# Long convolution, modulation and mixer MLP on one core: last inverse stage split per PSUM buffer, gelu table loaded early, loads regrouped on one queue, all tasks in a new order

## The chip, the core and the metric

The kernel runs on one core of a Trainium2 chip. A core has a matmul engine (TensorE, PE in the profile), a vector engine (VectorE, DVE), a scalar engine with function tables (ScalarE, ACT), a general engine (GpSimd, POOL) and a sync engine that issues transfers (SyncE, SP). Each engine works through its own queue in order; they wait for each other by semaphores. Matmuls write to PSUM, and ACT or DVE carries the results from there to SBUF, which is called eviction here. Transfers are issued from SP or POOL and carried by 16 DMA engines. The metric is the device time of one execution in microseconds (us), less is better.

## The reference

Everything is bf16, with S = 2048 positions and D = 640 channels. `rfft2` and `irfft2` over axes (1, 2) with one of them of length 1 are FFTs of length 2S along the positions.

```python
mod = (_silu(c) @ w_mod).reshape(c.shape[0], 6, 1, -1)
sa, ca, ga, sb, cb, gb = (mod[:, i] for i in range(6))
h = _layernorm(x) * (1 + ca) + sa              # x = A_q
x = x + ga * A(h, k, v)
h = _layernorm(x) * (1 + cb) + sb
x = x + gb * B(h)

def A(q, k, v):
    kv = shift(k, shift_k) * v                 # causal filter of 4 taps along S
    y = irfft(rfft(kv, 2 * S) * rfft(ssm_k, 2 * S))[:S]
    return q * (y + kv * ssm_D)

def B(x):
    h = gelu(_layernorm(x) @ w1)
    hs = concat(four quarters of h, shifted by +1, -1, +2, -2 positions) @ w2
    x1 = x + hs
    return x1 + gelu(_layernorm(x1) @ w3) @ w4     # w3: 640 x 1728
```

## The kernel before

**Stages.** The positions form 16 tiles of 128. The convolution is an FFT of length 4096 done with matmuls, in five blocks of 128 channels. A first stage with a 32-point matrix (`stage1`, matmuls L407) and a second with a 64-point matrix (`stage2_half`, matmuls L427) transform the filter (called s, result in R3) and the product kv (result in R5). In front of it stand the tables of sines, loads with transposes of k and v, and the filter of four taps by matmuls (L463). `inverse1` multiplies the two spectra on DVE (20 products of 128 x 2048, L617) and does the first inverse stage in matmuls (L628, L629). Every second product needs the filter's spectrum with its two halves of partitions exchanged; two transfers of 256 KB, one from SP and one from POOL, make it (`RK<-R` and others, L613), the "half swaps". `inverse2` is the last inverse stage: 512 matmuls of 32 x 32 x 160 (L661) for all 16 tiles, taken in six tasks of two or three tiles. It reads T0/T1 and RH; RH is filled by sixteen copies of 64 KB from RK (`RH<-RK`, L576), which may be issued from SP or POOL.

**From y to the MLP.** For each tile, `chain_a` multiplies y by the modulated q (`make_q`, L592 to L602, ring RQ) and adds x, with the sum and the square sum (L729, on ACT) as by-products; `ln_finish` turns these into mean and scale with some steps on POOL (L712 to L717); `chain_b` applies the second modulation, `chain_c` the MLP's first layernorm and turns the tile by PE (L772, copied from PSUM at L778/L780) or by a transfer from SP (L765). Then come w1 and gelu (`mm_w1`: L818 and L820 for the main part, L828 and L834 for the rest of each quarter), the shifted w2 (`mm_w2`: L873, L880), w3 with gelu (`mm_w3`: L907, L911) and w4 (`mm_w4`: L937, L928, L960), and output by SP (L969). The six vectors of the modulation come from twelve half loads of w_mod and 12 groups of matmuls (`mod_half`, L487, L493, L500 to L508); the statistics of x for the first layernorm are `ln1_stats` (on DVE two statistics instructions and an aggregation, L539/L540; on ACT two activations that accumulate, L547/L548).

**Order.** Every piece of work is a task that is added with its engine or a choice of engines, its reads and writes, and its PSUM slots. A string, ORDER, then lists all 1046 tasks in the order in which they are issued, each with a letter for the engine (S, P, A, D, G for SP, PE, ACT, DVE, POOL) and, for a task that takes PSUM, the digits of its slots. There are four slots of two banks each. A task must stand behind all tasks that it depends on; apart from this the order is free, and it fixes each engine's queue. The waits themselves come from the buffers that instructions share.

**What the change touches.** `inverse2` takes two slots for a task, because one task fills both halves of the channel blocks (j4 = 0, 1 and 2, 3), and both evictions depend on it. The loads of w1 and w2 (L992 to L995) and of x tiles 8 to 15 (`x_load`, L525) carry `r=y0`: they are made to stand behind the first tiles' evicted y, in Rb. The first gelu in ACT's queue is one of L834, and the function table is loaded in front of it.

Of the kernel before, what the change touches and what calls it, by code (L numbers as in the profile page):

```python
# [15 lines left out]
S, D, F = 2048, 640, 1728  # L16
# [10 lines left out]
0S 2S 19G 18D 50G 20D 21G 23D 22D 25A 4S 3S 1S 6S 27G 29D 36G 37G 28D 5S 8S 9S 11S 68G 10S 69D 24A 26G 88P:0 72G 73D 31A 30A 32D 38G 66D 89A 84P:1 85A  # L27
67D 90P:2 91A 86P:3 87D 39G 40A 102P:0 103A 100P:1 76P:2 70G 104P:0 41D 49G 101A 77A 42G 43G 105A 106P:3 107A 44A 45G 33S 47S 46S 71D 34S 12S 35S 48S
184S 181S 183S 182S 13S 14S 116P:1 92P:2 98P:0 74D 75D 117D 7S 99A 118P:3 119D 114P:0 15S 112P:1 113D 93A 110P:2 16S 115A 111A 96P:3 97A 94P:0 95D
82P:2 83A 80P:1 81A 78P:3 108P:0 51D 109A 52D 54A 56G 57D 53A 122P:2 79D 155P:1 156A 153P:0 154A 151P:3 152A 123D 157P:2 136D 120P:1 121D 173P:0 158A  # L30
55G 174A 171P:3 172A 177P:2 178D 175P:1 176A 161P:0 162D 141P:3 142A 167P:2 168D 147P:1 148A 58G 59G 163P:0 164D 165P:3 166A 137P:2 138A 145P:1 146A
230D 17S 149P:0 150A 190D 188D 126P:3 127D 139P:2 140A 60A 143P:1 199S 144A 124P:0 125D 179P:2 180A 187D 169P:3 170A 234P:1 235A 244P:2 159P:0 160A
128P:3 231D 242P:1 243A 245A 130P:0 61G 62G 186D 63G 64A 238P:1 239A 129D 131D 232D 248P:2 65G 196S 249A 246P:3 247A 185D 189G 191A 252P:0 202S 253A
134P:1 135D 132P:2 133D 236P:3 240P:1 237A 260P:0 261A 233D 250P:2 251A 241D 423D 200P:3 201A 258P:0 259D 319G 208S 192G 268P:2 269A 318S 197P:3 205S
198A 266P:1 267A 272P:2 273D 270P:3 271A 203P:0 284P:1 285A 292P:2 211S 204D 278P:3 279A 417D 276P:0 277A 342S 293D 426D 209P:1 210D 294P:2 295D 226S
290P:3 222G 291A 280P:1 281D 229G 227S 264P:0 274P:2 275D 343G 223G 265A 256P:3 262P:1 420D 206P:0 207D 257A 225G 254P:2 255D 282P:3 263A 286P:0
288P:1 287D 224G 312P:2 220S 283A 289A 212P:3 321D 320D 218G 213D 313A 328D 304P:0 305A 308P:1 316P:2 317A 217S 216G 302P:0 219S 214G 418D 228S 298P:2
215S 324P:3 325D 309A 221G 327G 326S 329D 322P:1 303A 336D 306P:0 299A 421D 323A 310P:2 296P:3 307A 334S 335G 337D 350S 297A 311A 300P:1 330P:0 301A
351G 332P:3 344D 345D 331A 314P:2 333A 315A 359G 340P:1 341A 338P:0 352D 348P:3 349A 353D 346P:2 358S 347A 360D 361D 354P:1 367G 339A 356P:3 368D 366S
369D 355A 364P:2 357A 375G 362P:0 376D 372P:1 374S 377D 401S 193A 363A 382S 370P:3 373A 384D 383G 385D 380P:0 378P:1 365A 392D 390S 391G 393D 422D  # L40
419D 424D 402P:2 427D 194D 403D 371A 388P:3 381A 379A 407S 389A 428D 386P:0 387A 416G 425D 396P:1 397A 394P:3 395A 398S 399P:0 400D 432P:12 429A 430D
434D 433A 489D 502A 510D 195G 413S 490D 491A 511D 530D 408P:3 513D 404S 405P:0 406A 531D 409A 512A 440S 492G 494D 475P:12 476A 477A 515D 532A 462P:03
463A 410S 411P:1 493G 495D 514G 435S 533D 534G 496A 497D 498G 441G 535D 464A 516D 536D 518D 499D 412A 517A 469P:20 537A 471A 519G 500P:3 538D 539G
414P:1 465G 470A 558D 449S 501D 520D 521P:3 436S 415A 507P:0 522A 443S 559D 560A 540D 541P:2 437S 542A 466P:13 431D 561D 562D 563A 564D 508A 546P:2
467D 468A 547A 548P:1 565G 448S 570D 528P:0 571D 566D 572D 567D 549A 573A 446S 568D 505P:3 506A 569A 574G 575G 447S 509G 529A 503D 523D 504D 621D 622D
472P:21 473A 526P:3 527A 623A 579D 580P:0 581A 576D 439S 543A 524D 577P:2 525D 624D 578D 625D 444S 438S 550P:3 627D 480S 551D 481S 626A 590P:0 591A
445S 482S 552A 588P:2 589A 595P:3 459D 628G 633D 629D 634D 553G 630D 631D 632A 635D 637D 636A 479S 554G 555D 556P:0 557A 592P:2 486S 596D 597A 638G
641A 639D 478S 488G 610P:3 612P:0 611A 593D 608P:2 606P:3 544D 594A 598D 613A 599G 474D 460A 603D 600D 601P:1 604P:0 609A 457D 607A 442S 454A 602A
640S 642S 651P:2 649P:3 461G 650A 450D 487S 652A 485S 605D 673P:0 667P:1 451D 545D 668A 674A 452G 582D 583D 484S 689D 690D 456A 458G 584D 585D 656P:3
692D 693D 653P:2 483S 614P:1 654D 655A 657D 694A 615D 659G 658A 671P:0 695D 660G 664D 665P:2 691A 661D 662P:3 663D 453D 669P:1 696G 701A 702D 703D  # L50
666A 735P:3 455G 672A 670A 697D 698D 699D 705G 737P:2 736A 739P:0 733P:1 616D 704A 643D 644D 645D 700A 738A 706G 709A 675P:32 710S 586D 587D 740A 755D
756D 757A 646A 707D 708S 758D 759D 717P:0 714D 761G 760A 762G 734A 763A 767D 777A 768D 711A 769D 719P:1 764D 780D 676P 718A 720A 721P:0 724P:1 647D
712D 765D 766A 677D 678D 770A 680S 771G 772G 683D 741P:32 648D 773D 774S 722D 775A 776S 785P:0 725D 726A 783P:1 713D 723A 824D 617S 825D 742P 821D
822D 827D 679S 681S 826A 743D 682S 727G 728G 731D 732S 823A 784A 828G 829A 786A 787P:3 729D 730S 833D 834D 835D 830D 831D 832A 837D 684D 685S 836A
620S 838G 790P:1 788D 789A 839D 840S 799P:0 791D 805P:3 806A 781D 841D 715D 716D 881D 749D 793G 792A 882D 842S 883A 803P:1 804A 794G 795A 796S 845P:2
846A 797D 778D 779D 884D 843P:3 844A 885D 887D 800A 801P:1 802A 618S 847P:2 848D 782D 941D 850P:3 851D 852A 886A 849A 619S 687S 798S 865P:0 866A
859P:1 860A 863P:2 807P:30 861P:1 744D 750D 753S 942D 944D 745S 853D 854G 855A 888G 893A 943A 752S 857A 889D 864A 945G 890D 856S 808P 858S 809D 891D
946A 947D 948D 950D 894D 862A 892A 895D 896A 897G 925P:2 926A 898G 751S 815D 747S 919P:3 901D 686S 920A 923P:1 899D 921P:0 949A 951G 922A 902S 900S
905P:2 906A 688S 903P:3 904A 952D 953S 956P:0 957A 954P:2 955A 907P:3 908D 910P:0 810D 958G 748S 959P:2 911D 913G 746S 816D 819S 924A 962P:1 867P:30
960D 817S 963D 813S 754S 912A 993P:2 909A 914G 812S 868P 915D 916S 917D 918S 977P:1 978A 994D 995A 996G 997G 971P:2 820S 972A 869D 998A 875D 927P:30  # L60
818S 964A 814S 811S 876D 961A 965D 966G 973P:1 967A 999S 969A 970S 870D 929D 974A 1028P:2 930D 975P:3 928P 968S 1000P:1 1001A 931S 935D 1002P:0 934S
976A 979P:13 981D 1003A 1006P:0 871S 873S 1004P:1 879S 1005A 872S 874S 936D 980P 987D 1029A 937S 933S 1026P:1 939S 1007A 877S 932S 988D 1024P:2 1025A
1032D 880S 878S 982D 983S 1008P:30 986S 991S 1027A 989S 1033D 1010D 938S 940S 1022P:2 1011D 1023A 1014S 1013S 1009P 1016D 984S 985S 1017D 1030P:13
1034D 992S 990S 1015S 1012S 1018S 1019S 1020S 1035D 1037S 1036S 1021S 1038S 1031P 1040D 1039S 1041D 1043A 1045A 1042S 1044S
# [72 lines left out]
def kernel(  # L137
# [57 lines left out]
    def ca(n):  # L195
        return 0.17 + 0.00083 * n
# [117 lines left out]
    def turns_to(dst, xs, n, r, w, neg=False):  # L314
        sc = (-2.0 if neg else 2.0) * PI_LO
        add("ACT", 0.23 + 0.00083 * n, lambda e: nc.scalar.activation(dst, xs, ACT.Sin, scale=sc), r=[r], w=[w])

    def sin_to(dst, ms, q, n, r, w, neg=False):
        b = (b_neg if neg else b_pos)[dst.start_partition():dst.start_partition() + dst.shape[0], :]
        sc = (2.0 if neg else -2.0) * PI_LO / q  # L320
        add("ACT", 0.25 + 0.00095 * n, lambda e: nc.scalar.activation(dst, ms, ACT.Sin, scale=sc, bias=b),
            r=[r, ("consts", 0, 1)], w=[w])
# [326 lines left out]
    def inverse2(tilesA):  # L649
        n = len(tilesA)  # L650
        pss = [Slot() for _ in range(2)]

        def f(e):
            for s in pss:
                pst(s, name="ps_i2")
            for a, A in enumerate(tilesA):
                for j4 in range(4):
                    for cg in range(4):
                        n1 = 4 * A + cg
                        for cpp in range(2):  # L660
                            nc.tensor.matmul(pss[j4 // 2].tile[32 * cg:32 * cg + 32, j4 % 2, a * 160:(a + 1) * 160],  # L661
                                             lhsT=Hs[32 * j4:32 * j4 + 32, n1, cpp, :],
                                             rhs=Zb[32 * j4:32 * j4 + 32, cpp * 64 + n1, :, :],
                                             start=(cpp == 0), stop=(cpp == 1), tile_position=(32 * j4, 32 * cg))
# [414 lines left out]
```

## Time and profile before

| | |
|---|---|
| device time, median of 3 runs | 302.04 us (301.63 to 302.31) |
| span of the profiled execution | 298.7 us, from its first to its last instruction |
| busy: PE / DVE / ACT / POOL | 269.7 / 218.2 / 208.3 / 104.8 us |
| mean granted TensorE clock | 0.975 |
| DMA moved | 35.76 MB, 120 GB/s in the mean |

The device time of the profiled execution itself is not listed; its span stands beside the median, which is 3.3 us longer. The rows of the profile below are the busy share of each of 40 equal slices (7.5 us each) in tenths; PEclk is the granted clock in tenths.

```profile
PE   0999999999989766869999999999999999999993
DVE  8998999999999998898759589886361544212442
ACT  4799989999999789979868775766854705431200
POOL 5864364453216591434275426120421321100000
PEclk9999999999999859799999999999999999999999
DMA  6999999898999920563700203223113030510112
```

Lines such as `L207 ACT CAST T<-ps_s 128x1024 ... x32 | 30.4, 1029 | 3.2 <-PE` give a group of instructions: line, engine, operation, what it writes and reads, how many, their busy time and the mean in ns, and the engine's idle time ahead of them with what ended most of it.

### The profile page before, as it was taken

How to read it: one execution, taken by the hardware profiler on the slowest of the kernel's cores; microseconds unless marked ns; L12 is line 12 of the kernel's file. 1: busy time of each engine (PE TensorE's matmuls, PEld its weight loads, DVE VectorE, ACT ScalarE, POOL GpSimd, SP SyncE). 2: the span in 40 equal slices, each digit the busy share in tenths (PEclk: the TensorE clock that was granted, in tenths of full speed). 3: DMA queues.
4: the chain of work that ended last, by engine and by line, in shares of the span. 5: the costliest groups of instructions: out<-in, count | busy, mean ns of one | idle time of the engine just before them, and what ended most of it. 6: DMA issues, size and time to landing. Idle time of an engine off the chain costs nothing.

```text
span 298.7 us, 7890 instructions
## 1 busy us (share of the span) xinstructions
PE 269.7 (90%) x3176; PEld 208.5 (70%) x3182; DVE 218.2 (73%) x438; ACT 208.3 (70%) x341; POOL 104.8 (35%) x237
## 2 busy tenths in 40 slices
PE   0999999999989766869999999999999999999993
PEld 0666755777878436648878677787788767887871
DVE  8998999999999998898759589886361544212442
ACT  4799989999999789979868775766854705431200
POOL 5864364453216591434275426120421321100000
PEclk9999999999999859799999999999999999999999
DMA  6999999898999920563700203223113030510112
GB/s 215 275 215 184 225 137 246 225 217 221 229 253 281 280 65 2 153 203 69 273 4 0 46 5 68 56 46 60 41 40 80 5 89 6 63 43 23 29 52 60
DMA packets 58356, 35.76 MB, mean 120 GB/s; under 512 B 40032, under 2 KB 55008, under 8 KB 58320
## 3 DMA queue, kind: packets, MB, share of 16 engines
q1 hardware_dynamic: 57136, 32.01, 46.3%
q0 software_dynamic: 1088, 3.21, 4.1%
q8 instruction: 25, 0.41, 0.6%
q14 instruction: 11, 0.09, 0.1%
q10 hardware_dynamic: 96, 0.04, 0.1%
HBM read 16.31 MB, written 2.62 MB: 63 GB/s over the span
## 4 chain that ended last, share of the span: by engine, by line
PE 51%; DVE 13%; ACT 11%; DMA 10%; POOL 6%; issue 5%; SPq 2%; DVEq 0%; POOLq 0%; ACTq 0%
PE ps_w L937 17%; PE ps_w L907 14%; ACT T L207 5%; DMA Ra<-in_A_q_dram 5%; PE ps_w L873 4%; PE ps_w L818 3%; PE ps_s L427 3%; ACT RG L729 3%; DVE Rb L617 3%; PE ps_ksh L463 2%; POOL lnv L715 2%; PE ps_s L407 2%; DMA RK<-R 2%; DVE R L756 2%; PE ps_mod L493 2%
## 5 line engine op out<-in xcount | busy, mean ns | idle before, releaser
L907 PE MATMUL ps_w<-R,T 128*128 128x256 bf16 (+1 forms) x630 | 63.8, 261 | 0.7 <-DMA R<-RH 0.7
L907 PEld LDWEIGHTS <-T 128*128 128x128 bf16 x630 | 55.5, 98 | 7.9 <-issue 2.0
L937 PE MATMUL ps_w<-T,R 128*128 128x320 bf16 x416 | 59.1, 299 | 0.0
L911 ACT ACTIVATE R<-ps_w 128x1024 bf16<-128x1024 f32 (+2 forms) x36 | 28.8, 827 | 41.9 <-PE ps_w L907 41.9
L937 PEld LDWEIGHTS <-R 128*128 128x128 bf16 x416 | 40.5, 98 | 15.2
L960 DVE TENSOR_TENSOR T<-ps_w,R 128x640 bf16<-128x640 f32 x15 | 12.3, 822 | 35.4 <-PE ps_w L928 18.1
L207 ACT CAST T<-ps_s 128x1024 bf16<-128x1024 f32 x32 | 30.4, 1029 | 3.2 <-PE ps_s L407 3.1
L207 ACT CAST R<-ps_s 128x960 bf16<-128x960 f32 (+1 forms) x35 | 30.8, 964 | 1.8 <-PE ps_s L427 1.6
L407 PE MATMUL ps_s<-F1bd,Rb 128*128 128x256 bf16 x160 | 23.3, 298 | 8.7 <-DVE Rb L394 8.1
L729 ACT ACTIVATE RG<-R 128x640 bf16<-128x640 bf16 x32 | 23.5, 734 | 9.9 <-DVE R L880 6.7
L407 PEld LDWEIGHTS <-Rb 128*128 128x128 bf16 x160 | 16.7, 107 | 14.7 <-DVE Rb L394 8.6
L873 PE MATMUL ps_w<-RG,R 128*128 128x320 bf16 x160 | 23.2, 299 | 2.1 <-ACT R L820 2.1
L715 POOL TENSOR_TENSOR lnv<-lnv,mhalf 128x2 f32<-128x2 f32 (+1 forms) x29 | 22.5, 775 | 2.3
L427 PE MATMUL ps_s<-T,RG 64*128 64x160 bf16 x512 | 21.2, 230 | 0.8 <-ACT R L207 0.6
L880 DVE SCALAR_TENSOR_TENSOR R<-ps_w,R 128x640 bf16<-128x640 f32 x16 | 12.9, 819 | 11.8 <-PE ps_w L873 11.6
L427 PEld LDWEIGHTS <-RG 64*128 64x128 bf16 x512 | 17.7, 94 | 5.1 <-issue 4.6
L818 PE MATMUL ps_w<-R,RG 128*128 128x256 bf16 (+1 forms) x200 | 20.0, 259 | 1.3 <-DMA R<-RK 0.6
L873 PEld LDWEIGHTS <-R 128*128 128x128 bf16 x160 | 15.4, 98 | 8.2 <-ACT R L820 2.4
L629 PE MATMUL ps_i<-EB,Rb 128*128 128x128 bf16 x160 | 19.0, 219 | 1.5 <-DVE Rb L617 1.4
L818 PEld LDWEIGHTS <-RG 128*128 128x128 bf16 x200 | 17.1, 102 | 3.5 <-issue 2.0
L628 PE MATMUL ps_i<-EA,Rb 128*128 128x128 bf16 x160 | 19.0, 219 | 0.4 <-ACT R L207 0.3
L714 POOL TENSOR_TENSOR lnv<-stat,lnv 128x2 f32<-128x2 f32 x19 | 4.0, 212 | 40.9 <-ACT RG L729 28.7
(178 smaller groups left out, 513.5 us busy)
## 6 DMA issues: line engine op xcount, KB each, us to landing
Ra<-in_A_ssm_k_dram SPq DMA_DIRECT2D x5, 512.0 KB, 5.7
R<-in_w_mod_dram SPq DMA_DIRECT2D x6, 400.0 KB, 6.0
out_dram<-RH SPq DMA_DIRECT2D x60, 40.0 KB, 1.6
T<-in_B_w_dram SPq DMA_DIRECT2D x5, 432.0 KB, 6.2
RH<-in_w_mod_dram SPq DMA_DIRECT2D x4, 400.0 KB, 4.4
Ra<-in_A_q_dram SPq DMA_DIRECT2D x4, 320.0 KB, 6.6
RK<-R SPq DMA_DIRECT2D x5, 256.0 KB, 4.5
RK<-R POOLq DMA_DIRECT2D x5, 256.0 KB, 5.3
```

The source lines that it names most:

```text
L207: nc.scalar.copy(dst, src(ps.tile))
L407: nc.tensor.matmul(psv[:, ml, :], lhsT=xL[:, s0:s0 + P], rhs=F1r, start=True, stop=True)
L427: nc.tensor.matmul(psv[:, g, j], lhsT=Gs[p, k, 64 - 64 * cc:192 - 64 * cc], rhs=T1h[h][p, cc * 32 + k], start=(cc == 0), stop=(cc == 1), t ...
L628: nc.tensor.matmul(psv[:, w, :], lhsT=Av[:, r_, :, g_], rhs=EAf, start=True, stop=False)
L629: nc.tensor.matmul(psv[:, w, :], lhsT=Bv[:, r_, :, g_], rhs=EBf, start=False, stop=True)
L715: nc.gpsimd.tensor_tensor(rs, rs, mhalf[:, 0:n], ALU.pow)
L729: add("ACT", 0.74, lambda e: nc.scalar.activation(junk, src, ACT.Square, scale=float(D) ** -0.5, accum_out=stat[:, li, 1, t:t + 1]), r=[sk ...
L818: nc.tensor.matmul(pt[:, fb, 0:cw], lhsT=w1_sb[:, b, 160 * fb:160 * fb + P], rhs=hT[:, b, 0:cw], start=(b == 0), stop=(b == ND - 1))
L873: nc.tensor.matmul(pt[:, hf, 0:320], lhsT=gsf[:, fb, c0:c0 + P], rhs=w2_sb[:, fb, 320 * hf:320 * hf + 320], start=(fb == 0), stop=(fb == 4))
L907: nc.tensor.matmul(pt[:, fl, 0:cw], lhsT=w3_sb[:, b, fb * P:(fb + 1) * P], rhs=xT[:, b, 0:cw], start=(b == 0), stop=(b == ND - 1))
L911: nc.scalar.activation(g3[g % 2][:, f0:f0 + fn, 0:cw], ps.tile[:, 0:fn, 0:cw], ACT.Gelu_apprx_tanh)
L937: nc.tensor.matmul(bank(i, hf), lhsT=gg[:, fb, i * P:(i + 1) * P], rhs=w4_sb[:, fb, 320 * hf:320 * hf + 320], start=(fb == 0 and i == 0), ...
```

## The change

Five things are changed.

1. `inverse2` makes two PE tasks for each group of tiles, one for each PSUM slot, with 32 matmuls a tile instead of 64; each eviction depends on its own task alone. Matmuls and evictions are the same.
2. A new ACT task applies gelu to one column of `b_pos`. All sine activations write a region "sin" that it reads, so that it stands behind them all, and all gelus read the region "gelu" that it writes. In the new order it stands in ACT's queue behind the square sum of tile 1's `chain_b`, ahead of an eviction of the last inverse stage.
3. `r=y0` is gone from the loads of w1, w2 and x tiles 8 to 15. In the new order the late halves of w_mod, four of the eight x pieces, w2 and w1 are issued during the inverse products; the other four x pieces stand behind the loads of w3.
4. The sixteen copies into RH all have the letter S: before, seven were on SP and nine on POOL. One half of each swap stays on POOL.
5. ORDER is new as a whole. The tasks number 1053 now. Where a task may be on two engines, 28 went from ACT to DVE, 36 from DVE to ACT, 12 from POOL to DVE and 6 from DVE to POOL.

```diff
@@ ORDER @@
 (all lines of ORDER replaced)
...
     def turns_to(dst, xs, n, r, w, neg=False):
         sc = (-2.0 if neg else 2.0) * PI_LO
-        add("ACT", 0.23 + 0.00083 * n, lambda e: nc.scalar.activation(dst, xs, ACT.Sin, scale=sc), r=[r], w=[w])
+        add("ACT", 0.23 + 0.00083 * n, lambda e: nc.scalar.activation(dst, xs, ACT.Sin, scale=sc), r=[r], w=[w, ("sin", 0, 1, "s")])
...
     def inverse2(tilesA):
         n = len(tilesA)
-        pss = [Slot() for _ in range(2)]
-
-        def f(e):
-            for s in pss:
-                pst(s, name="ps_i2")
-            for a, A in enumerate(tilesA):
-                for j4 in range(4):
-                    for cg in range(4):
-                        n1 = 4 * A + cg
-                        for cpp in range(2):
-                            nc.tensor.matmul(pss[j4 // 2].tile[32 * cg:32 * cg + 32, j4 % 2, a * 160:(a + 1) * 160],
...
-        t1 = add("PE", 0.38 * n, f, r=[("T01", 0, 20480), ("RH", 0, 4096)], alloc=tuple(pss), act=0.2, ni=64 * n)
         yv = y_all[:, tilesA[0]:tilesA[0] + n, :].rearrange("p a (j u) -> p j a u", j=4)
         for i in range(2):
-            t2 = evac(yv[:, 2 * i:2 * i + 2], lambda t: t[:, :, 0:160 * n].rearrange("p j (a u) -> p j a u", a=n), 320 * n, pss[i],
+            ps = Slot()
+
+            def f(e, ps=ps, i=i):
+                pt = pst(ps, name="ps_i2")
+                for a, A in enumerate(tilesA):
+                    for jj in range(2):
+                        j4 = 2 * i + jj
+                        for cg in range(4):
+                            n1 = 4 * A + cg
+                            for cpp in range(2):
+                                nc.tensor.matmul(pt[32 * cg:32 * cg + 32, jj, a * 160:(a + 1) * 160],
...
+            t1 = add("PE", 0.2 * n, f, r=[("T01", 0, 20480), ("RH", 0, 4096)], alloc=ps, act=0.2, ni=32 * n)
+            t2 = evac(yv[:, 2 * i:2 * i + 2], lambda t: t[:, :, 0:160 * n].rearrange("p j (a u) -> p j a u", a=n), 320 * n, ps,
                       [("Rb", D * tilesA[0], D * (tilesA[0] + n), "y")])
             dep(t2, t1)
...
     E0 = 64 + S
+    add("ACT", 0.25, lambda e: nc.scalar.activation(s64[:], b_pos[:], ACT.Gelu_apprx_tanh),
+        r=[("consts", 0, 1), ("sin", 0, 1)], w=[("gelu", 0, 1), ("scol", 0, 1)])
...
-                 w=[("gs", t0_, t0_ + n, "gs"), ("R3", 0, 5 * GW, "gs")], use=ps)
+                 r=[("gelu", 0, 1)], w=[("gs", t0_, t0_ + n, "gs"), ("R3", 0, 5 * GW, "gs")], use=ps)
...
     inverse2([0, 1, 2])
-    y0 = [("Rb", 0, D)]
-    dma("SP", 800, lambda q: q.dma_start(w1_sb, B_w1.rearrange("(b p) n -> p b n", p=P)), r=y0, w=[("RG", 0, 3200)])
-    dma("SP", 700, lambda q: q.dma_start(w2_sb[:, 0:4, :], B_w2.rearrange("(g r) n -> r g n", g=4)[0:P]), r=y0, w=[("RG", 3200, 6400, "w2")])
+    dma("SP", 800, lambda q: q.dma_start(w1_sb, B_w1.rearrange("(b p) n -> p b n", p=P)), w=[("RG", 0, 3200)])
+    dma("SP", 700, lambda q: q.dma_start(w2_sb[:, 0:4, :], B_w2.rearrange("(g r) n -> r g n", g=4)[0:P]), w=[("RG", 3200, 6400, "w2")])
...
-    x_load(8, 12, y0)
-    x_load(12, NT, y0)
+    x_load(8, 12)
+    x_load(12, NT)
```

## The prediction

> **What bounds the kernel now.** I read three views in this order: the table of stretches (busy time of each engine in chosen stretches of the span), the waits of each engine, and the timelines where a wait looked removable. I cut the span at four events of the timelines: 53.59, the last transposed slot of the convolution's input; 93.79, the last DVE product of the inverse (L617); 135.7, the first matmul with w3 (L907); 293.9, the last PE work.
>
> ```profile
> core 0: us, PE busy (x) PEld busy (x) DVE busy (x) ACT busy (x) POOL busy (x), PEclk, DMA share, GB/s
> 0.00:53.59 53.59, 44.49 (x450) 29.54 (x457) 50.36 (x80) 44.80 (x57) 30.31 (x47) 1.00 1.03 216
> 53.59:93.79 40.20, 37.65 (x621) 31.99 (x619) 39.72 (x42) 39.28 (x48) 13.52 (x27) 1.00 0.92 226
> 93.79:135.70 41.91, 31.05 (x728) 22.81 (x729) 38.12 (x101) 37.01 (x76) 22.39 (x58) 0.84 0.53 153
> 135.70:293.90 158.20, 156.46 (x1380) 124.17 (x1378) 89.15 (x215) 87.18 (x163) 38.61 (x108) 1.00 0.24 53
> 293.90:298.70 4.80, 0.09 (x1) 0.00 (x0) 0.81 (x2) 0.00 (x0) 0.00 (x0) 0.85 0.17 44
> ```
>
> The reader is to see four regimes in it. Up to 93.79 DVE and ACT are full (from 53.59 on DVE idles 0.48 of 40.20 us, ACT 0.92), so there every microsecond of their work counts. From 93.79 to 135.7 nothing is quite full: DVE idles 3.79, ACT 4.90, PE 10.86, and PE runs at a mean clock of 0.84. From 135.7 PE is full (idle 1.74 of 158.20), and its matmuls there are the same in both kernels. So the end is the first w3 matmul plus about 163 us (298.7 - 135.7), and the change can win only by an earlier first w3 matmul, by a part of those 1.74 us, or in the tail.
>
> What holds PE back between 53.59 and 135.7, in the view of its waits:
>
> ```profile
> engine line waited for: us in total, times, longest us
> PE ps_i L661 <- issue: 3.3, 2, 1.8
> PE ps_w L873 <- ACT R L820: 2.1, 1, 2.1
> PE ps_i L629 <- DVE Rb L617: 1.4, 5, 0.3
> PE ps_w1x L828 <- ACT R L834: 1.2, 1, 1.2
> ```
>
> L661 are the last inverse stage's matmuls; "issue" is a stop for which the profile shows no releaser. Both stops (before 101.45 and 108.20) lie in the middle of a group of these matmuls, while DMA is at its fullest. L828 waiting for L834 is the gelu table:
>
> ```profile
> 115.56 1.28 ACT L834 ACT_TABLE_LOAD   x1
> 116.85 1.10 ACT L834 ACTIVATE R<-ps_w1x 32x128 bf16<-32x128 f32 x4
> ```
>
> And the chain of waits passes, right after the products, through SP and two loads of x that are released only then:
>
> ```profile
> 93.85 0.47 SPq L992
> 94.32 0.05 issue
> 94.37 8.41 DMA Ra<-in_A_q_dram
> 102.81 5.34 DMA Ra<-in_A_q_dram
> ```
>
> **What the Trainium skill says.** "ScalarE: Activation LUTs", section "What ACT_TABLE_LOAD costs", gives 1283 ns for the load and 1380 ns for a drain, 2.66 us a switch. The trace agrees on the load (1.28 us) but shows no drain: the next ACT instruction starts at 116.85, 0.01 us after it. I use 1.28. "DMA: Bandwidth & Descriptors", section "Issuing engines are not separate DMA queues", says that transfers issued from several engines share the same 16 DMA engines, and that spreading the issue saves only issue time. The trace fits: a half swap takes 4.5 us from SP and 5.3 from POOL. So moving issues to SP costs their issue time and what they stand in front of, no bandwidth. "Perfetto Trace Analysis", section "Optimization Strategy", says to take a kernel with several regimes by regime, and to look at the gaps of the full engine in each; hence the cut above.
>
> **The change part by part.** The new order is a list of the same tasks, so I counted the tasks by engine in each stretch in both lists and priced each move with durations of this trace: eviction of 1024 columns ACT 1.03 / DVE 1.22, of 960 0.96 / 1.15, of 640 0.67 / 0.80; statistics of one x tile ACT 1.7 / DVE 1.08; normalization ACT 0.92 / DVE 0.44; copy of a turned tile 0.68 / 0.475.
>
> (1) Work moved between ACT and DVE. 28 tasks go from ACT to DVE and 36 the other way, and seven small layernorm steps go from POOL to DVE. Priced, DVE has 1.8 us less up to 53.59, 0.9 less from there to the last product, and 0.3 more from there to the first w3 matmul; ACT has 1.8 more, 1.0 more and 1.5 more. Up to 53.59 I take zero: the last slot waits for the k and v transposes, which come over SP in unchanged order. In the second stretch DVE has 0.48 us of idle time, so its 0.9 less could be worth up to -0.9; but ACT with 1.0 more has only 0.92 of idle. I take -0.3, ends -0.9 and +0.8. In the third stretch the floors are 38.1 + 0.3 = 38.4 (DVE) and 37.0 + 1.5 = 38.5 (ACT), against 41.9 now: at most -3.4, if all idling ended.
>
> (2) Last inverse stage split. The same 512 matmuls and 12 evictions, in 12 PE tasks of one PSUM slot instead of 6 of two. Each eviction can begin after half as many matmuls (a group of 96 takes 1.20 us, so about 0.6 us sooner), and a group need not find two free slots. No instruction is added. Alone worth 0 to -1, inside the floor of (1).
>
> (3) Gelu table early. One column of gelu is added on ACT between the second square sum and an eviction (estimate 0.2 us: the smallest ACT rows, a read of the accumulator, take 0.19), and brings the 1.28 us load with it. The load stays on ACT, at a place where the next gelu doesn't stand behind it; PE's 1.24 us before L828 goes. What is late next are the gelus themselves, which stand in ACT's queue behind square sums and evictions. 0 to -1.2. Queued behind the load now is an eviction of the last inverse stage, with PE matmuls of other slots beside it: up to +0.5 if no slot is free.
>
> (4) Loads. w1, w2 and the late x tiles no longer wait for the first evicted y; the w_mod halves, the first x pieces, w2 and w1 are all issued during the inverse products. The 8.41 and 5.34 us pieces of the chain are thus begun before 93.79, and less DMA traffic lies over the last inverse stage, where PE's two stops of 3.3 us are. In that stretch an instruction queue of three packets stands beside 2.5 MB of loads; if the stops are late instructions, they go, up to -3.3, again inside the floor of (1). The other four x pieces now stand behind w3 (issued when the last inverse matmul is done); a statistics task on ACT waits for one of them. In the trace before, w3 was issued at 122.21 and all landed by 132, so pieces behind it land about 135 to 138: 0, or up to +2 if ACT stands there with gelus behind it.
>
> (5) All sixteen copies RH<-RK (L576) on SP. Nine were on POOL, where they held that queue for 5.7 us (a wait for a mod matmul). On SP one takes about 0.61 us (0.59 plus a gap). Eleven of them come after the mod matmul that frees RH (65.6 us before; some 1.5 earlier in the new list): 11 x 0.61 = 6.7, the last issued near 71, landed 3.3 later near 74.3. Behind them in SP's queue stand SP's halves of the swaps (L613): the one for the second block issued near 71.3, landed 4.9 later at 76.2; the third block's source is complete at 74.3, landed at 79.2. DVE's queue from that mod matmul to the second block's product holds seven evictions (8.05), two products (2.28), two mod updates (0.98), two halves of q (0.97) and a normalization (0.44): 12.7 us, so it comes there near 77.2, and to the third block's product three products later, near 80.6. Covered by 1.0 and 1.4 us; if transfers come 2 to 3 us later than that, DVE, full here, stands 1 to 2 us at each.
>
> **The sum.** 0 (to 53.59) - 0.3 (to 93.79) - 1.5 (third stretch) - 0.5 (a part of the 1.74 us of PE idle after 135.7; ends -1.7 and +1.5, as the new order may also stop PE where the old didn't) = -2.3. I take 1.5 of the 3.4 us in the third stretch: it would have DVE and ACT busy 38.4 and 38.5 of 40.4 us, 95%, and engines that wait for each other in a chain (product, square sum, POOL's power, normalization, turn) will hardly reach the 99% of the stage before. The profiled span is 298.7; the median of the three runs is 302.04, so about 3.3 us lie around it. 302.0 - 2.3 = 299.7.
>
> **The rivals.** A: all stops go. PE's 3.3 and 1.2 us vanish, ACT and DVE run full to the first w3 matmul: -0.9 - 3.4 - 1.0 = -5.3, 296.7. For it: the stops are in a stretch where no engine is full. Against: the chains of small steps there. B: nothing. The first w3 matmul is held by the ACT and DVE work in front of it, and what PE gains it waits for elsewhere: 302.0. C, on the slower side: ACT's load. ACT gets 1.0 + 1.5 = 2.5 us more between 53.59 and 135.7, and if it idles as before (0.92 + 4.90), the first w3 matmul comes 2.5 us later: 304.5. It decides when ACT's idle time in the third stretch stays over 3.4 us (4.90 - 1.5). For it: ACT is the engine that both square sums and gelus wait for, and it alone gets more work in every stretch. D, also slower: SP's queue. The copies and swaps land 2 to 3 us late, DVE stands about 3 us before the second and third product, and a third of it is won back: 304. That the change doesn't do what it says is seen only in (2) and (4): the split helps nothing if slots were not what the evictions waited for.
>
> **Numbers.** Likeliest case 299.7, chance 0.40; A 0.15; B 0.09 (within 0.2%, which is 0.6 us and about what a measurement of this kernel can tell from no change); C 0.24; D 0.12. Faster 0.55, same 0.09, slower 0.36. The range 296.0 to 305.0 takes in A and C with their margins; the likeliest case alone has 298.0 to 301.3.
>
> **What would show it.** First L907 at 133.9 (right), 135.7 (B), 138 (C). The idle time of ACT between the last product and it: 2 to 3 us in mine, over 3.4 in C. The two stops of L661 gone, and no ACT_TABLE_LOAD between a w1x matmul and its gelu. DVE waits on RK<-R over 2 us mean D. PE idle after the first L907 over 2.5 us would make the prediction wrong although its first half were right.

## The result, and the profile after

The changed kernel takes 303.82 us in the median of 8 runs (303.00 to 305.09), the kernel before 301.92 us beside it (301.05 to 303.03): a ratio of 1.0057, 95% interval 1.0029 to 1.0085. It is slower by some 1.7 us, where 2.3 us less was forecast. The profiled execution spans 301.5 us against 298.7. The second of these is a quick one. In all runs that list both, the device time is 1.66 to 2.15 us longer than the span, 1.7 in the median, so a span of 298.7 us belongs to a device time near 300.4, and no other listed execution of the kernel before has a shorter span. The 3.3 us that the prediction puts around the span are therefore about half a difference between executions.

The table of stretches, of the changed kernel, is cut at the same four events as before: the last transposed slot of the convolution's input, the end of the last product, the first w3 matmul, the end of the PE work.

```profile
core 0: us, PE busy (x) PEld busy (x) DVE busy (x) ACT busy (x) POOL busy (x), PEclk, DMA share, GB/s
0.00:55.73 55.73, 44.66 (x461) 29.44 (x462) 52.32 (x77) 47.58 (x65) 29.86 (x53) 1.00 0.99 214
55.73:99.02 43.29, 36.74 (x615) 31.65 (x614) 38.78 (x40) 39.36 (x48) 10.22 (x17) 1.00 0.91 209
99.02:139.65 40.63, 31.00 (x729) 24.15 (x730) 37.58 (x99) 37.66 (x79) 21.52 (x51) 0.83 0.69 180
139.65:296.80 157.15, 156.55 (x1380) 124.00 (x1377) 86.69 (x221) 94.02 (x170) 38.39 (x101) 1.00 0.23 46
296.80:301.50 4.70, 0.14 (x1) 0.00 (x0) 0.82 (x2) 0.00 (x0) 0.00 (x0) 0.98 0.18 44
```

The length of each row is its second number. Against before (53.59, 40.20, 41.91, 158.20, 4.80) the first stretch is 2.1 us longer, the second 3.1 us longer, the third 1.3 us shorter, the fourth 1.05 us shorter and the tail 0.1 us shorter: together +2.8, the difference of the two spans, of which about 1 us is not in the device times and comes from the quick execution before. So the change did gain what was forecast for it behind the products, and lost more ahead of them. In the second stretch DVE's work fell as counted (38.78 against 39.72), but its idle time rose from 0.48 to 4.51 us. The view of DVE's waits, in and just ahead of that stretch, names what it waited for (us in total, times, longest us):

```profile
DVE modv L501 <- PE ps_mod L494: 2.1, 1, 2.1
DVE Rb L618 <- DMA RK<-R: 1.2, 1, 1.2
DVE modv L503 <- PE ps_mod L494: 0.7, 1, 0.7
```

Lines are one to three higher than before (L618 is the product, L494 the modulation matmul, L501 and L503 its updates on DVE). In the kernel before, the same view of this stretch lists nothing. Two queues stand behind these waits. One is the modulation: a PE group waited 1.9 us for a load of w_mod into RH, and DVE's update stood in its queue where it had to wait for that group. The other is SP's, in the chain of waits of the changed kernel:

```profile
59.10 7.57 DMA RK<-in_w_mod_dram
66.69 0.51 SPq L577
67.24 0.59 SPq L577
...
71.30 1.08 SPq L577
72.42 2.04 DMA RH<-RK
74.54 6.99 DMA RK<-R
```

The reader sees SP issue one copy into RH after another (L577), the last of the sixteen landing at 74.46, then SP's half of the third block's swap, issued at 74.54 and landing 6.99 us later. Before, SP issued the same half at 70.97 and it landed 3.4 us later, as the view of the transfers issued there shows, before and after (size, then us to landing):

```profile
RK<-R SPq DMA_DIRECT2D x1, 256.0 KB, 3.4
RK<-R SPq DMA_DIRECT2D x1, 256.0 KB, 7.0
```

POOL's half took 5.3 us before (issued at 71.24) and 5.1 after (issued at 74.11). In the changed kernel SP's half is the last of four halves of swaps that SP and POOL issue between 73.11 and 74.54, three of them from SP.

### The profile page after: what moved, and what is told of

The parts are those of the page before. It is cut to its first block, busy times and chain, and to the rows that moved or that the text cites. A ratio compares the mean times of both kernels' runs of the same rounds, so it can differ in the third digit from the quotient of the medians.

```text
span 301.5 us, 7925 instructions
## 1 busy us (share of the span) xinstructions
PE 269.1 (89%) x3182; PEld 209.2 (69%) x3182; DVE 216.2 (72%) x438; ACT 218.6 (73%) x359; POOL 100.0 (33%) x220
## 4 chain that ended last, share of the span: by engine, by line
PE 62%; DVE 14%; DMA 13%; issue 3%; ACT 3%; SPq 3%; POOL 0%; DVEq 0%; POOLq 0%
PE ps_w L910 19%; PE ps_w L940 18%; PE ps_w L876 6%; DMA RK<-R 5%; PE ps_w L821 5%; PE ps_ksh L464 4%; DVE Rb L395 3%; DMA T<-in_B_w_dram 3%; DMA RK<-in_w_mod_dram 3%; PE ps_s L408 2%; PE ps_s L428 2%; SPq L577 2%; DVE Rb L618 2%; DMA Ra<-in_A_ssm_k_dram 1%; DVE R L757 1%
## 5 line engine op out<-in xcount | busy, mean ns | idle before, releaser
L940 PEld LDWEIGHTS <-R 128*128 128x128 bf16 x416 | 40.3, 98 | 15.9 <-issue 0.8
L208 ACT CAST T<-ps_s 128x1024 bf16<-128x1024 f32 x33 | 31.6, 1029 | 1.5 <-PE ps_s L408 1.3
L408 PE MATMUL ps_s<-F1bd,Rb 128*128 128x256 bf16 x160 | 22.1, 286 | 10.7 <-DVE Rb L395 9.3
L208 ACT CAST R<-ps_s 128x960 bf16<-128x960 f32 (+1 forms) x31 | 27.3, 988 | 2.6 <-PE ps_s L428 2.6
L716 POOL TENSOR_TENSOR lnv<-lnv,mhalf 128x2 f32<-128x2 f32 (+1 forms) x29 | 21.7, 749 | 2.3
L821 PE MATMUL ps_w<-R,RG 128*128 128x256 bf16 (+1 forms) x200 | 21.1, 269 | 1.2 <-DVE R L781 1.2
L821 PEld LDWEIGHTS <-RG 128*128 128x128 bf16 x200 | 18.2, 107 | 3.0 <-issue 1.7
L208 ACT CAST T<-ps_i 128x1024 bf16<-128x1024 f32 x20 | 18.9, 1056 | 1.5 <-PE ps_i L630 1.0
```

The costliest lines, as they stand in the source:

```text
L208: nc.scalar.copy(dst, src(ps.tile))
L408: nc.tensor.matmul(psv[:, ml, :], lhsT=xL[:, s0:s0 + P], rhs=F1r, start=True, stop=True)
L716: nc.gpsimd.tensor_tensor(rs, rs, mhalf[:, 0:n], ALU.pow)
L821: nc.tensor.matmul(pt[:, fb, 0:cw], lhsT=w1_sb[:, b, 160 * fb:160 * fb + P], rhs=hT[:, b, 0:cw], start=(b == 0), stop=(b == ND - 1))
L940: nc.tensor.matmul(bank(i, hf), lhsT=gg[:, fb, i * P:(i + 1) * P], rhs=w4_sb[:, fb, 320 * hf:320 * hf + 320], start=(fb == 0 and i == 0), ...
```

## The experiments

Each run is compared with runs of the kernel before on the same chip; a ratio is followed by its 95% interval. The stretches come from one profiled execution of each. Edits of ORDER are shown as the tasks moved.

**e1 and e2: the first stretch exchanged.** Tasks are taken in the order and with the engine letters of the other kernel up to the last slot.

```diff
 e1, the changed kernel:
-ORDER, changed, up to 259A
+ORDER of before, up to 241D, then the rest as changed
 e2, the kernel before:
-ORDER of before, up to 233D
+ORDER, changed, up to 259A, then the rest as before
```

> The changed kernel, with its first 221 tasks (all up to the last transposed slot of the convolution's input) in the order and on the engines of the kernel before; the rest as changed. Theory 1 (the new order of the first stretch costs the 2.1 us by which the last slot came later, 55.73 against 53.59): the slot is back at 53.6 +-0.5 and the time falls by about 2 us, to the time of before (+-0.8). Theory 2 (the loss is in the second stretch: the copies and swaps in SP's queue, the waits for the modulation matmuls): the slot comes earlier, but DVE then waits the longer for the modulation matmuls, and the time falls by under 0.7 us.

> The kernel before, with its first 225 tasks in the order and on the engines of the changed one. Theory 1: the last slot comes at 55.7 +-0.5 and the time rises by about 2 us. Theory 2: the slot comes late, but the second stretch takes part of it back, the time rises by under 0.7 us.

e2: 304.02 us, ratio 1.0069 (1.0049 to 1.0089), with the slot at 56.71 and the stretches behind it 40.14, 41.95 and 162.7: the new first stretch costs about 2.1 us by itself. Over all runs with an unaltered first stretch, the slot comes at 53.56 to 54.92 in the old order (seven profiles, mean 54.1) and at 55.73 to 57.13 in the new one (five profiles, mean 56.35). e1 missed: the slot came back to 54.31, but the time rose to 305.46 us, ratio 1.0103 (1.0067 to 1.0138), since the second stretch grew to 47.6 us. DVE's waits there, in e1:

```profile
DVE modv L501 <- PE ps_mod L494: 4.8, 1, 4.8
DVE Rb L618 <- DMA RK<-R: 3.0, 2, 2.3
```

Both waits of the changed kernel are there, larger, but the first not for the same reason. No PE group waits for a load in this stretch of e1, and while DVE stood there (57.66 to 62.44) PE's granted clock was 0.50 for 3.41 us:

```profile
58.23:61.64 3.41, 3.17 (x15) 1.88 (x14) 0.00 (x0) 3.00 (x5) 0.00 (x0) 0.50 0.65 165
```

How much of the 4.8 us is the clock's and how much the order's stays open. In e1 the early slot gained nothing, with the modulation update and the swaps in DVE's way. So the first stretch is not the whole cause: theory 1 holds for the kernel before (e2). In the changed one (e1) DVE waits longer, as theory 2 says, but neither theory had the time rise.

**e3 and e9: what in the first stretch.** In the changed kernel DVE's 512-wide table instructions take 939 and 1193 ns in the mean, against 541 and 427 before, with POOL's table instructions beside them. e3 puts them apart; e9 restores the engine letters of 25 tasks of the first stretch and leaves their places.

```diff
 e3:
-0S 18D 19G 56G 20D ... 29D 25A ... 57G ... 72D 28D 53A ... 39G
+0S 18D 19G 20D ... 29D 28D 25A ... 72D 53A ... 39G 56G 57G
 e9:
-77D 140D 144D 152D 160D 172D 243D 79A 95A ... 42D 58D 61D
+77A 140A 144A 152A 160A 172A 243A 79D 95D ... 42G 58G 61G
```

> The changed kernel with three tasks moved in the first 11 us: DVE's second pair of 512-wide table instructions directly behind its first, as in the kernel before, and POOL's 512-wide table instructions for the third table later. If these DVE instructions were slow (0.94 and 1.19 us in the mean against 0.54 and 0.43) because POOL works beside them, they take 2 us less together, the first transposed slots come 1 to 2 us earlier, and the time falls by 1 to 2 us. If DVE's start doesn't set the later stages, the time stays within 0.5 us.

> The changed kernel with the engines (not the places) of 25 tasks of the first stretch as in the kernel before: six evictions and one first eviction of kv back from DVE to ACT, five evictions and three x statistics the other way, the small table steps between POOL and DVE as before. If the new engines set the late slot (56.5 in the mean of the runs with the new front, 54.2 with the old): it comes 1.5 to 2.5 us earlier, the time falls 0.5 to 2 us, less what the modulation matmuls and swaps behind it then wait longer. If the new places set it (table instructions beside POOL's, order of products and slots): the slot stays at 56 to 57, the time within 0.5 us.

e3: the instructions became fast again, as the groups of DVE's first 12 us show (busy us, then mean ns), the changed kernel first, then e3:

```profile
L294 DVE TENSOR_SCALAR R<-R 128x512 int32<-128x512 int32 x2 | 2.4, 1193 | 0.1
L293 DVE TENSOR_SCALAR R<-R,s,offc 128x512 int32<-128x512 int32 x2 | 1.9, 939 | 0.0
```

```profile
L293 DVE TENSOR_SCALAR R<-R,s,offc 128x512 int32<-128x512 int32 x2 | 1.1, 538 | 0.0
L294 DVE TENSOR_SCALAR R<-R 128x512 int32<-128x512 int32 x2 | 0.9, 426 | 0.1
```

The second and third transposed slots ended at 12.6 instead of 14.6, and yet the last slot came at 56.80 and the time was 303.92 us, ratio 1.0046 (1.0028 to 1.0065), the changed kernel's within the intervals. DVE's waits for the k filter's matmuls were 2.8 us instead of 1.4, but they were 3.2 in e2, which has the changed first stretch as it is, so this is not e3's doing. What made the instructions slow can be seen in the timelines of DVE and POOL in the changed kernel (start, length):

```profile
9.16 1.26 POOL L311 TENSOR_TENSOR R<-R 128x512 f32<-128x512 f32 x1
9.20 1.51 DVE L294 TENSOR_SCALAR R<-R 128x512 int32<-128x512 int32 x1
```

Each of the four ends about 0.28 us after the POOL instruction beside it, as if it did most of its work only then. In e2 POOL's instructions lie a little otherwise, and DVE's second pair took 0.54 and 0.71 us in place of 0.95 and 1.51 (POOL's instruction beside it took 2.20 in place of 1.96), with the slot late all the same. e9: slot at 59.37, 307.80 us, ratio 1.0191 (1.0163 to 1.0219). For e3 the second of its two cases came true, and e9 fell outside both of its own: engines of the one order in the places of the other are worse than either kernel. Which single move makes the slot late stays open.

**e4 and e7: the second stretch of the changed kernel.** e4 gives nine copies back to POOL. e7 moves the modulation matmul that waits for its load behind three groups of the second stage, with its update behind one eviction.

```diff
 e4:
-214S 216S 218S 221S 222S 223S 224S 225S 229S
+214G 216G 218G 221G 222G 223G 224G 225G 229G
 e7:
-206P:1 ... 292P:3 ... 274P:2 ... 221S ... 207D ... 276P:1 ... 275D
+292P:3 ... 274P:2 ... 276P:1 206P:0 221S ... 275D 207D
```

> The changed kernel with nine of the sixteen copies RH<-RK back on POOL, as before; all places in the order kept. Theory 2 (SP's queue): copies all issued some 3 us earlier (last near 69 in place of 72.4), the third block's swap 2 to 3 us earlier, DVE's 1.2 us wait for it gone, the time down by 1 to 2 us. Theory 1: the time stays within 0.5 us, since other waits hold DVE.

> The changed kernel; the modulation matmul that waits 1.94 us for its load is moved behind three groups of the second stage on PE, and its DVE update behind one eviction; the PSUM slots of ten groups rotated to fit. If the modulation chain (load, matmul, next load) holds DVE only by its place in the queues: DVE's 2.1 us wait goes, products end 1 to 2 us earlier, the time falls 1 to 2 us. If the copies and swaps behind that matmul hold the products: DVE waits longer for RK<-R instead, and the time changes by under 0.5 us.

e4: the second stretch fell to 41.18 us and DVE's wait for RK<-R went, though not by the way expected: SP's half of the third block's swap was issued at 75.58, later than in the changed kernel, and took 4.5 us in place of 7.0; 303.36 us, ratio 1.0026 (1.0007 to 1.0045) against the change's 1.0057 (1.0029 to 1.0085). The intervals overlap, so the gain of some 0.9 us is likely, not shown. e7: 2.1 us of waiting for L501 gone, 1.0 us for the other update and 0.7 for the swap left, the second stretch 41.51; but the slot of this profile came at 57.13, and the time was 304.51 us, ratio 1.0085 (1.0054 to 1.0115): no gain. A gain of 2 us in the stretch of one profile is not much by itself: e3, which changes nothing there, has 42.09 against 43.29. In the changed kernel neither queue alone is shown to carry the loss.

**e6 and e12: the copies in the old order.** All sixteen copies on SP, nothing else, in the kernel before (e6), and in e2 (e12).

```diff
 e6, e12:
-214G 216G 218G 221G 222G 223G 224G 225G 229G
+214S 216S 218S 221S 222S 223S 224S 225S 229S
```

> The kernel before with all sixteen copies RH<-RK on SP, nothing else. Theory SP queue: the copies take 10 to 13 us of SP, the swap for the third block lands 2 to 3 us later, DVE waits 1 to 3 us on RK<-R in a stretch where it is full, the time rises by 1 to 2.5 us. Rival (POOL's relief and DVE's own queue cover it): within 0.5 us.

> Run e2 (the kernel before with the changed order up to the last slot) with all sixteen copies RH<-RK on SP as well: both suspects in the old order of everything behind. If they add up, 302.5 + 2.1 (e2) + 4.2 (e6), some 308 to 309, and the changed kernel's 303.8 then says that its new order in the second stretch wins some 2.5 back beyond the 2 us of its later stretches. If the late slot covers the copies (they wait for the same modulation matmuls), the second stretch is 41 to 42 us and the time 304 to 306.

e6: 306.63 us, ratio 1.0156 (1.0118 to 1.0193): this one part, put into the old order, costs more than the whole change, and more than expected. The stretches of e6 and DVE's waits in it:

```profile
0.00:53.71 53.71, 44.10 (x456) 28.59 (x457) 50.24 (x80) 44.71 (x57) 30.37 (x47) 1.00 1.03 217
53.71:98.47 44.76, 39.14 (x621) 33.36 (x619) 39.92 (x42) 39.97 (x49) 9.04 (x18) 0.96 0.87 202
```

```profile
DVE Rb L617 <- DMA RK<-R: 3.6, 1, 3.6
DVE Rb L617 <- PE ps_i L628: 0.9, 2, 0.6
```

The second stretch grows from 40.20 to 44.76 us, 4.56, and DVE stands 3.6 us for the second block's swap and 0.9 behind it for PE, whose granted clock was 0.50 from 79.19 to 82.60. In this stretch, where DVE is full, the 4.5 us that it stands come out as 4.56 at its end. The third stretch is 0.9 us longer too (42.83), which is not explained. The copies lie at 61.81 to 74.38 in SP's queue instead of 61.68 to 68.67, and SP's half of the second block's swap behind them is issued at 74.48 instead of 68.77; it then landed in 3.0 us, before in 3.4. So DVE's wait here comes from the issuing and not from the transfer. e12: 310.11 us, ratio 1.0280 (1.0242 to 1.0318); the second stretch is 45.77. The two losses add up (1.0069 and 1.0156 would give 1.0226, and up to 1.0284 by their intervals). The changed kernel has both and takes 1.0057: its new order in the second stretch, and the stretches behind it, win about 2.2% back.

**e8, e5, e10 and e11: where the gain is.** e8 is the kernel before with the split and the early table alone. e5 is the old order up to the last product and the new one behind it. e10 has the new order only from the first w3 matmul on. e11 is e5 with ten loads of w1, w2 and x behind the first evicted y again.

```diff
 e8, the code as changed, ORDER of before in the new numbers:
-inverse2 P:12
+inverse2 P:1, inverse2 P:2
+432A behind the square sum of tile 1's chain_b
 e5:
-ORDER, changed, up to 393D
+ORDER of before, up to 393D
 e10:
-ORDER, changed, up to the first mm_w3
+ORDER of before, up to the first mm_w3
 e11, in e5:
-448S 446S 442S 441S 444S 447S 438S 439S 440S 437S ... 434A
+434A 448S 446S 442S 441S 444S 447S 438S 439S 440S 437S
```

> The kernel before with two parts of the change alone, in its own order: the last inverse stage split per PSUM buffer (each pair of new tasks in the place of the old one, same slots), and the gelu table loaded behind tile 1's second square sum. The 1.24 us wait of a w1x matmul for the table goes; first w3 matmul 0.5 to 1.5 us earlier, the time down by 0.3 to 1.5 us. If ACT sets the first w3 matmul, the load costs it the same 1.28 us wherever it stands, and the time stays within 0.5 us.

> The changed kernel with all tasks up to the last product of the spectra (392 of them) in the order and on the engines of the kernel before, copies included; from there on as changed (one mod eviction, 379, placed before a mod matmul for its PSUM slot). If the whole loss is in the first two stretches and the 1.3 and 1.05 us gained after the products stand by themselves: last product ends at 93.8 to 94.5, first w3 matmul about 40.5 to 41 later, the time 1 to 2.5 us under the kernel before (300 to 301.5 where that is 302.5). If the gain was only work and loads shifted out of the first stretches, first w3 comes as before or later, and the time is that of before or more.

> The kernel before up to its first w3 matmul (split of the last inverse stage included, gelu table loaded at the first gelu, loads as before), from there the changed order. The gain of the last stretch alone: 161.9 in place of 163.0 us from the first w3 matmul to the end, the time 0.6 to 1.5 us under before. If that gain was only work moved ahead of the first w3 matmul, 163 us again and the time of before.

> Run e5 (old order to the last product, new order behind it) with ten of the early loads, of w1, w2 and x, placed behind the first evicted y again, as before. If the early loads carry e5's gain: first w3 matmul 1 to 2 us later and the time back at that of before. If not: within 0.5 us of e5.

e8: 302.63 us, ratio 1.0004 (0.9983 to 1.0025), third stretch 41.98: the split and the early table are worth nothing that can be told in the old order (0.5 us at most, by the interval). e5: 300.37 us, ratio 0.9933 (0.9910 to 0.9956), faster than both kernels. Its stretches:

```profile
0.00:54.53 54.53, 44.66 (x456) 28.78 (x457) 50.18 (x81) 44.96 (x57) 30.35 (x47) 1.00 1.05 213
54.53:95.10 40.57, 36.71 (x603) 30.93 (x602) 39.69 (x42) 38.88 (x47) 13.55 (x27) 1.00 0.93 232
95.10:136.70 41.60, 32.24 (x751) 25.28 (x749) 37.52 (x98) 38.70 (x80) 22.54 (x53) 0.84 0.66 169
136.70:298.60 161.90, 156.67 (x1380) 124.05 (x1377) 87.52 (x223) 94.07 (x170) 38.73 (x101) 1.00 0.23 48
```

The first two are those of before again, and the last (tail included) is 161.9 us, as in the changed kernel, against 163.0. The third is only 0.3 us shorter than before. e11: 300.05 us, ratio 0.9951 (0.9932 to 0.9971), third stretch 42.08, last 161.7: no part of the gain can be seen to come from the early loads. PE's stops in L661 for no releaser shown, which the prediction tied to DMA traffic, are 3.5 us in e8 and 0.4 in e5, and none is listed in e11, where these loads are late again: they go with the order. In their place PE waits 3.2 us (e5) and 3.6 us (e11) there for evictions by ACT. e10: 305.26 us, ratio 1.0127 (1.0092 to 1.0162), with this in PE's waits behind the first w3 matmul:

```profile
PE ps_w L910 <- ACT Rb L208: 2.8, 1, 2.8
```

That is an eviction of the last inverse stage, which I had to place ahead of a w3 group for its PSUM slot; it takes back what the last stretch was to show (164.9 us with the tail). e10 tells nothing on the last stretch alone.

One profile of each kernel says little on a difference of 1 us, so here are the means over all profiles that have a stretch in the old or in the new order, without e1's second stretch and e10's last: 54.1 and 56.35 us for the first (seven and five profiles), 40.3 and 42.7 for the second (six and three), 42.2 and 41.2 for the third (six and eight), 163.3 and 162.1 for the last with its tail (five and eight). The differences are +2.2, +2.4, -1.0 and -1.1, together +2.5; the ratio's interval is 0.9 to 2.6 us.

## Why the prediction was wrong

The forecast was the sum 0 - 0.3 - 1.5 - 0.5. The profile of the changed kernel gives +2.1, +3.1, -1.3 and -1.15 with the tail; the means over the profiles give +2.2, +2.4, -1.0 and -1.1. Two steps failed, the zero for the first stretch and the -0.3 for the second.

*First stretch, "Up to 53.59 I take zero: the last slot waits for the k and v transposes."* This failed. The transposes came no later (SP issued the last one until 47.59, before until 48.05, and it landed at 49.8, before at 50.4), and the slot still came 2.1 us later. Between landing and slot there is a queue of DVE instructions: the slot follows the last landing by 3.1 to 4.0 us in the seven profiles of the old order and by 5.7 to 6.2 us in the five of the new one. So what came later is DVE's queue, not the load. In the old order the transposes do play a part: in five of the seven profiles DVE stands 0.5 us or more for a load of v near 40 us. I had seen DVE busy 50.36 of 53.59 us and taken the rest of its wait for a transfer's. Also "DVE has 1.8 us less" was wrong by 3.8: its busy time ahead of the slot was 52.32, up 1.96, of which 2.3 us are the four table instructions that ran slow beside POOL; the other 1.4 us of the error are not traced. A count of tasks prices them alike. The Trainium skill, "SBUF — State Buffer", section "SBUF: two separate sides", does say that DVE and POOL share a pair of ports that, for some modes of DVE's instructions, one holds for a whole instruction while the other blocks; the slow instructions beside POOL's, which end about 0.28 us after them, and the fast ones in e3 (1193 and 426 ns) fit that (no run shows which mode they are in), and I should have looked where the moved ones come to lie. e2 shows that the new first stretch costs about 2 us; e3 shows that the slow instructions are not what the slot waits for.

*Second stretch, "-0.3, ends -0.9 and +0.8".* This failed, by more than its ends. The -0.9 of work came (-0.94), and 4.0 us of waits came with it. For SP's copies the working of part (5) was close: the product of the second block started at 76.97 (77.2 in the text), the last copy landed at 74.46 (74.3), DVE reached the third block's product at 80.45 (80.6). But SP's half of its swap took 6.99 us where I had put 4.9 (before it took 3.4; a piece of 4.90 us in the chain there belongs to POOL's half), and "covered by 1.4 us" became a wait of 1.2: rival D, at less than half of its price. The other 2.8 us, DVE waiting for modulation matmuls, I had not priced at all. I followed the copies behind that matmul and not the DVE updates that it feeds, nor that the load for it came 7.2 us after its issue. e1 shows both waits growing to 7.8 us together when the slot comes early, a part of it perhaps by PE's clock; e6 shows that the copies on SP cost 4.2 us in the old order. Which share of the second stretch's loss each wait has in the changed kernel stays open, since e4 and e7 each took one away without a gain in time that is clear of the noise.

*Third stretch, -1.5.* Right in size: -1.3. That is in part luck, since its reasons were half right. The wait of a w1x matmul for the table is gone (ACT_TABLE_LOAD stands at 114.11, with a 0.20 us gelu behind it), one of the two stops of L661 is left with 1.7 us, and ACT's idle time is 2.97 us, under the 3.4 at which rival C, ACT's load, would have decided. But e8 gives nothing for the split and the table alone, e11 nothing for the loads. The gain comes with the new order and is not theirs one by one. In e5 and e11, with the first two stretches in the old order, the stretch is 0.3 us shorter and 0.2 us longer than before. So part of the 1.3 us may be work that the changed kernel's longer first stretches had already taken.

*Fourth stretch, -0.5.* Right in sign, too small: -1.05, PE's idle time falling from 1.74 to 0.60 us. The three waits of 0.7, 0.6 and 0.5 us there, two of them for turned tiles, became 0.3 and 0.2.

*Issuing engines.* The Trainium skill, "DMA: Bandwidth & Descriptors", section "Issuing engines are not separate DMA queues", says that spreading the issue saves only issue time. In e6 this was so, and the issue time was what mattered: sixteen issues in one queue in front of a transfer that a full engine waits for, issued 5.7 us later and then no slower (3.0 us against 3.4). In the changed kernel the wait of 1.2 us came with a slower transfer as well (7.0 us).

## What to carry to other kernels

Where an engine is full, ask of every instruction in its queue who feeds it, not only of those that the change names: in the changed kernel the 2.8 us of waits that were not on the list were more than the 1.2 us of the one that was worked out. An engine that is busy 94% of a stretch is the first suspect for what ends it, ahead of the transfer that arrives a few us earlier. When a new order mixes a gain and a loss in different stretches, cut both orders at an event and join the halves: that gave versions 0.5 and 0.7% faster than the kernel before, the faster of the two, while four parts undone one at a time inside the new order (e3, e4, e7, e9) gave no gain clear of the noise or made it worse. Ask also how quick the profiled execution was against the median: here about 1 us of the 2.8 us between the two profiles came from that.

## What the runs showed that was not expected

DVE's 128x512 int32 table instructions took 0.43 us alone and 0.88 and 1.51 us beside POOL's 512-wide instructions (mean 1193 ns against 426 in e3), and each slow one ended about 0.28 us after POOL's. The same 256 KB from SP, its half of the third block's swap, took 3.36 us in the kernel before, 6.99 in the changed one, 4.54 in e4 and 4.03 in e6. In the runs where DVE stood longest in the second stretch, PE's granted clock fell there too: 0.96 in e6 and 0.93 in e1 and e12, against 1.00 in before and in the changed kernel. No run here separates what the lower clock adds to the waits from what the order does.
